# A three-stage model on one core: a third tile for queries and keys, the first load in two parts, four stores begun by GpSimd

## The chip, the cores and the metric

One core of a Trainium2 chip runs the whole program. The metric is the device time of an execution in microseconds; the time given is the median of the runs. One further execution was taken by the profiler; times with a position ("at 20.11") are microseconds from the start of its span.

## What is computed

Attention with a soft cap, then a feed-forward network with a LayerNorm ahead of it, then a gated network that mixes positions. Batch 4, 12 heads of 64, 448 positions, width 768, all float32:

```python
scores = cap * tanh(q @ k.T / 8 / cap)            # 448 x 448 for each of 48 heads
x   = softmax(scores) @ v                          # heads side by side: 4 x 448 x 768
x   = x + relu(layernorm(x) * g @ w_ch1) @ w_ch2   # 768 -> 3072 -> 768
u, v = halves(relu(x @ w_in))                      # 768 -> 1024
out = (u * (w_spatial @ layernorm(v) + b_spatial)) @ w_out
```

## The kernel before, in words

Two heads are worked on together, a "pair"; the program names it by its first head, so 0, 2, 4 and so on. For each pair there is one load of transposed queries and keys (`emit_load`, line 822: 128 rows, of which each head has 64, by 896 columns, queries in columns 0 to 447, keys behind) and two of values (`emit_load_v`, line 836). The pool of tiles for queries and keys, `qk`, has `FIRST[1]` = 2 tiles (line 47).

The lead is the attention of the first two batch elements, 12 pairs, in the first 100 us or so. `lead_s` (line 875) makes the scores of a pair in three groups of 128 keys, `two` and `t` in PSUM, and ScalarE turns them to `e` by a tanh and an exponential. `lead_st` (line 895) makes the last 64 keys of two pairs together. `lead_v` (line 906) multiplies `e` by the values and makes the sums over the keys: VectorE adds the groups of `e` to `es`, TensorE multiplies `es` by `onesr` and `sel`. `invert` (line 1001) takes the sums through DRAM to a shape of 128 rows (`sum`, then `rc`), VectorE takes reciprocals, and they go out and come back, spread over rows (`inv`, then `hs`); VectorE then multiplies `x` by `hs`. When the six pairs of a batch element are there, their LayerNorm follows, which begins with `bank<-wh,onesr` on TensorE; GpSimd takes a power there, with the constant `mhalf`.

Beside the lead, four rows of the first FFN matrix (`EARLY`, line 73) are made ready: `make` (723) calls `weight` (795), which calls `value` (738). A row is loaded as 64-bit words (`w`, two tiles), converted to float32 in four operations by VectorE, or three and one of ScalarE (`wr`, two tiles), stored to DRAM for later use (`kept_w`, line 753), and split in two parts of fewer bits (`rs` or `wh`). The other rows, and the second pair of batch elements, follow behind the lead, as do the two networks, most of the 1008.6 us.

No instruction stands where the code has it. All calls go through `Recorder`, which puts down for each operation its engine, a cost and, for a transfer, a latency (line 544, for SP alone, whose name here is "D"); line 561 issues it at last, so that all rows of the profile name L561. `order` (327) gives each operation a due time from TensorE's order and the costs, and `plan` (374) runs a list schedule with these costs and sets the order on every engine. Operations under `at_once` (the first loads, lines 1863 to 1867) come ahead of all others.

Of the kernel before, what the change touches and what calls it, by code (L numbers as in the profile page):

```python
# [43 lines left out]
FAST = 22,  # L44

COUNTS = 16, 10, 3, 2, 3, 1
FIRST = 2, 2, 2, 1
REST = 7, 10
LEAD = 2, 5

# [173 lines left out]
class Program:  # L224
# [102 lines left out]
    def order(self):  # L327
        n = len(self.ops)
        pred = self.edges()
        self.pred, self.succ = pred, [[] for _ in range(n)]  # L330
        for i, ds in enumerate(pred):
            for j, at in ds.items():
                self.succ[j].append((i, at))
        self.bufs = []
        for i, (_, writes, reads) in enumerate(self.ops):
            mine = list(dict.fromkeys(a.buf for a in chain(writes, reads) if isinstance(a, View)))
            for b in mine:
                b.first = i if b.first is None else b.first
                b.last = i
                b.uses += 1  # L340
            self.bufs.append(mine)
        self.pools = {b.pool for m in self.bufs for b in m}
        total = 0.0
        due = [float("inf")] * n
        for i in range(n):
            engine, cost = self.ops[i][0][0][:2]
            if engine == "PE":
                due[i] = total
                total += cost
            elif i in self.soon:  # L350
                due[i] = total
        for p in self.pools:
            p.reuse()
        for s in self.stages:
            begins = [b for p in s.pools for b in p.bufs if b.first is not None]
            if s.after and begins:
                first = min(begins, key=lambda b: b.first)
                for a in s.after:
                    for b in (b for p in a.pools for b in p.bufs if not b.after):
                        assert b.last < first.first  # L360
                        b.gates.append(first)
        for i in reversed(range(n)):
            engine, cost, latency = self.ops[i][0][0][:3]
            latency += 1.4 if engine == "D" else 0.0
            for j, at in chain(self.succ[i], {(a.first, 0.0) for b in self.bufs[i] for a in b.after},
                               {(a.first, -OPEN / SLACK) for b in self.bufs[i] for a in b.gates}):
                due[i] = min(due[i], due[j] + at * SLACK - (cost + latency + self.DELAY) * SLACK)
            if due[i] == float("inf"):
                due[i] = total
        for i in self.first:  # L370
            due[i] = float("-inf")
        return self.plan(due)

    def plan(self, due):
# [14 lines left out]
        out = []  # L389
# [59 lines left out]
        while True:  # L449
            for e in ready:  # L450
                if busy[e]:
                    continue
                found = pick(e)
                if found is None:
                    continue
                i, k = found
                taken[i] = True
                out.append((i, k))
                for b in bufs[i]:
                    if b.tile is None:  # L460
                        b.pool.take(b)
                busy[e] = True
                cost, latency = self.ops[i][0][k][1:3]
                if e == "PE":
                    spent += cost
                free[e] = now + cost
                if e == "D":
                    moved = max(moved, now + 1.5) + latency
                    latency = moved + 0.77 - now - cost
                heapq.heappush(events, (now + cost, 0, seq, e))  # L470
                done = now + cost + latency + self.DELAY
                for j, at in succ[i]:
                    heapq.heappush(events, (max(now, done - at), 1, seq, j))
                    seq += 1
                heapq.heappush(events, (done, 2, seq, i))
                seq += 1
            if not events:
                rest = [d for q in ready.values() for d, i, _ in q if not taken[i] and d > reach()]
                if not rest:
                    break  # L480
                relief = min(rest)
                continue
            relief = float("-inf")
            now, kind, _, x = heapq.heappop(events)
            if kind == 0:
                busy[x] = False
            elif kind == 1:
                left[x] -= 1
                if not left[x]:
                    release(x)  # L490
            else:
                for b in bufs[x]:
                    b.left -= 1
                    if not b.left:
                        b.pool.give(b)
                        if b.pool.stage is not None and not b.pool.stage.left:
                            for s in b.pool.stage.then:
                                if not s.open and all(not a.left for a in s.after):
                                    s.open = True
                                    out.append((s, None))  # L500
                                    for p in s.pools:
                                        p.changes += 1
                                    for p in s.more:
                                        p.idle.extend(p.late)
                                        p.changes += 1
# [16 lines left out]
class Recorder:  # L522
# [3 lines left out]
    def __getattr__(self, method):  # L526
        fn = getattr(self.engine, method)

        def put(a):
            return a.place() if isinstance(a, View) else a  # L530

        def record(*args, **kw):
            out = kw["out"] if "out" in kw else args[0]
            ins = [a for a in list(args) + list(kw.values()) if hasattr(a, "tensor") and a is not out]
            n = out.free_size()
            latency = 0.0
            psum_in = any(a.space == bass.MemoryType.PSUM for a in ins)
            if self.name == "PE":
                cost = (n / 2400 + 0.0133) * kw["rhs"].ap[0][1] / 128
                if kw["rhs"].dtype == F32:  # L540

                    part = kw["rhs"].ap[0][1] * kw["out"].ap[0][1] / 128 ** 2
                    cost = (4 * n / 2400 + 0.004) * part + (0.004 if part < 1 else 0.0)
            elif self.name == "D":
                cost, latency = 0.5, 4 * out.size() / 360e3
            elif self.name == "A":
                cost = (0.13 if psum_in else 0.16) + n / 1200
                cost += 0.094 if hasattr(kw.get("scale"), "tensor") else 0.0
            elif self.name == "P":
                cost = 1.3 if "pow" in repr(args) + repr(kw) else 0.7 + n / 500  # L550
            elif method == "reciprocal":
                cost = 0.15 + n / 160
            elif method in ("tensor_copy", "tensor_scalar") and not psum_in:
                cost = 0.14 + n / 1920
            else:
                cost = 0.14 + n / 960
            if self.name == "V":
                cost += 0.06 * sum(hasattr(kw.get(k), "tensor") for k in ("scalar", "scalar1", "scalar2"))

            def call():  # L560
                fn(*(put(a) for a in args), **{k: put(a) for k, a in kw.items()})  # L561

            self.program.add(self.name, cost, latency, call, [out], ins)

        return record
# [3 lines left out]
def attn_ffn_gmlp_kernel(  # L569
# [168 lines left out]
    def value(kind, j, home=None, pool=wr):  # L738
# [5 lines left out]
        elif (kind, j) in kept:  # L744
            t = pool.get()[:, 0:n]
            SP.dma_start(out=t, in_=kept[kind, j])
        else:
            raw = raw6[0].get()[:, 0:n]
            SP.dma_start(out=raw.rearrange("p n t -> p (n t)"), in_=source[kind][j].bitcast(I32))
            t = pool.get()[:, 0:n]  # L750
            convert(t, raw, home is None, kind in ("wv", "wu", "wo"))
            d = kept[kind, j] = dram.tile([128, n], F32, name=f"kept_{kind}_{j}")
            SP.dma_start(out=d, in_=t)
        return t

    def block(q, g, pool, early):
# [65 lines left out]
    def emit_load(i):  # L822
# [3 lines left out]
        b, h = heads[i]  # L826
        t = raws[i] = qks.get()

        SP.dma_start(out=t, in_=qk[b, h:h + 2].rearrange("a p n -> (a p) n")[64:192])

    def place(i):

# [1029 lines left out]
    def main():  # L1862
        with prog.at_once():
            emit_load(0)
            SP.dma_start(out=capt, in_=cap)
            emit_load(2)
            emit_load_v(0)
        SP.dma_start(out=g_t, in_=g_ln)
# [101 lines left out]
```

## Time and profile before

| | |
|---|---|
| median of 3 runs | 1011.92 us (1008.72 to 1013.71) |
| the profiled execution | 1010.37 us |
| its span, first to last instruction | 1008.6 us |
| TensorE, busy | 997.3 us |
| VectorE, ScalarE, GpSimd, busy | 855.2, 584.9, 16.7 us |
| granted clock of TensorE | 1.000 of 2.4 GHz all through |

Engines: PE is TensorE (PEld its weight loads), DVE VectorE, ACT ScalarE, POOL GpSimd, SPq the queue of SyncE, which starts transfers. A row of the timeline gives start, length, engine, line, operation, what is written from what, and how many; in brackets the idle time of the engine ahead of it and what ended it. A matrix product in float32 shows as two matmuls. Overlapped operations of an engine are shown with their whole length, so that the distance between two starts can be less than the length.

### The profile page before, as it was taken

How to read it: one execution, taken by the hardware profiler on the slowest of the kernel's cores; microseconds unless marked ns; L12 is line 12 of the kernel's file. 1: busy time of each engine (PE TensorE's matmuls, PEld its weight loads, DVE VectorE, ACT ScalarE, POOL GpSimd, SP SyncE). 2: the span in 40 equal slices, each digit the busy share in tenths (PEclk: the TensorE clock that was granted, in tenths of full speed). 3: DMA queues.
4: the chain of work that ended last, by engine and by line, in shares of the span. 5: the costliest groups of instructions: out<-in, count | busy, mean ns of one | idle time of the engine just before them, and what ended most of it. 6: DMA issues, size and time to landing. Idle time of an engine off the chain costs nothing.

```text
span 1008.6 us, 14721 instructions
## 1 busy us (share of the span) xinstructions
PE 997.3 (99%) x5108; PEld 827.7 (82%) x5108; DVE 855.2 (85%) x1425; ACT 584.9 (58%) x890; POOL 16.7 (2%) x22
## 2 busy tenths in 40 slices
PE   8999999999999999999999999999999999999998
PEld 2334787787788899998989889999999999998987
DVE  6767887888967899989889999877788988968996
ACT  7996955877775358656356355444453543314653
POOL 0000000000000000000000200000000000000010
PEclk9999999999999999999999999999999999999999
DMA  7546678988897998997386233565699857302402
GB/s 251 170 137 180 214 254 294 365 305 303 300 331 230 347 359 297 332 345 273 119 308 218 43 144 116 169 204 191 236 329 371 290 184 233 103 21 71 128 21 110
DMA packets 121197, 224.30 MB, mean 222 GB/s; under 512 B 20594, under 2 KB 83236, under 8 KB 121124
## 3 DMA queue, kind: packets, MB, share of 16 engines
q1 hardware_dynamic: 121124, 223.38, 65.1%
q8 instruction: 40, 0.66, 0.3%
q14 instruction: 33, 0.27, 0.1%
HBM read 152.76 MB, written 70.57 MB: 221 GB/s over the span
## 4 chain that ended last, share of the span: by engine, by line
PE 84%; DMA 6%; DVE 6%; issue 1%; ACT 1%; SPq 1%; DVEq 0%; ACTq 0%
PE bank L561 58%; PE two L561 26%; DMA w6m<-in_w_dram 2%; DVE rs L561 1%; DVE x L561 1%; DMA hs<-inv 1%; DMA std<-var_t 1%; DVE wh L561 1%; DMA w<-in_w_dram 1%; SPq L561 1%; PE t L561 1%; DVE qkg L561 1%; DMA wq<-kept_w 1%; DMA qk<-in_qk_dram 1%; DVE wr L561 1%
## 5 line engine op out<-in xcount | busy, mean ns | idle before, releaser
L561 PE MATMUL bank<-rs,wh 128*128 128x448 f32 x1728 | 362.9, 363 | 1.2 <-DVE rs L561 0.7
L561 PEld LDWEIGHTS bank<-rs,wh 128*128 128x128 f32 x1728 | 322.5, 187 | 29.5 <-issue 3.0
L561 PE MATMUL two<-rs,wh 128*128 128x448 f32 x462 | 103.7, 362 | 0.7 <-DVE wh L561 0.7
L561 DVE TENSOR_TENSOR rs<-hs,rs 128x448 fp32r<-128x448 f32 x159 | 94.3, 618 | 4.7 <-ACT rs L561 4.5
L561 ACT ACTIVATE rs<-hs 128x448 fp32r<-128x448 f32 x135 | 73.2, 570 | 32.7 <-DMA hs<-h 31.4
L561 PEld LDWEIGHTS two<-rs,wh 128*128 128x128 f32 x462 | 86.5, 187 | 6.9 <-DVE wh L561 1.0
L561 DVE TENSOR_TENSOR wh<-wr,wh 128x768 fp32r<-128x768 f32 (+2 forms) x66 | 57.4, 871 | 3.0 <-ACT wh L561 2.5
L561 ACT ACTIVATE hs<-bank 128x448 f32<-128x448 f32 x58 | 31.5, 543 | 40.1 <-PE bank L561 33.9
L561 ACT ACTIVATE wh<-wr 128x768 fp32r<-128x768 f32 (+2 forms) x44 | 33.7, 766 | 30.8 <-PE bank L561 16.6
L561 ACT ACTIVATE es<-es,capt 128x896 f32<-128x896 f32 x42 | 42.6, 1052 | 0.1
L561 ACT ACTIVATE hx<-bank 128x448 f32<-128x448 f32 x30 | 16.3, 543 | 39.2 <-PE bank L561 30.1
L561 PE MATMUL two<-qk 64*128 64x448 f32 (+1 forms) x168 | 36.1, 575 | 2.9 <-DMA qk<-in_qk_dram 2.0
L561 ACT ACTIVATE rs<-x 128x448 fp32r<-128x448 f32 x29 | 16.3, 575 | 36.5 <-DVE x L561 35.1
L561 PE MATMUL bank<-es,vt 128*64 128x448 f32 (+1 forms) x192 | 36.0, 551 | 0.0
L561 ACT ACTIVATE es<-two,qsc 128x896 f32<-128x896 f32 x32 | 31.5, 1007 | 6.3 <-PE two L561 6.3
L561 PE MATMUL two<-wh,rs 128*128 128x512 f32 x144 | 34.7, 389 | 0.0
L561 PE MATMUL bank<-rx,whb 128*128 128x448 f32 x144 | 32.7, 362 | 0.0
L561 PE MATMUL two<-rx,whb 128*128 128x448 f32 x144 | 32.7, 362 | 0.0
L561 DVE TENSOR_TENSOR es<-es,es 128x896 f32<-128x896 f32 x24 | 26.1, 1086 | 7.5 <-ACT es L561 7.5
L561 PEld LDWEIGHTS two<-qk 64*128 64x128 f32 (+1 forms) x168 | 11.3, 173 | 25.5 <-issue 9.1
L561 PEld LDWEIGHTS two<-wh,rs 128*128 128x128 f32 x144 | 27.0, 188 | 5.6
L561 ACT ACTIVATE e<-e,capt 128x2688 f32<-128x2688 f32 (+1 forms) x14 | 31.0, 2224 | 0.2
(268 smaller groups left out, 1966.1 us busy)
## 6 DMA issues: line engine op xcount, KB each, us to landing
hs<-h SPq DMA_DIRECT2D x168, 224.0 KB
h<-hx SPq DMA_DIRECT2D x84, 224.0 KB
w<-in_w_dram SPq DMA_DIRECT2D x24, 768.0 KB
qk<-in_qk_dram SPq DMA_DIRECT2D x24, 448.0 KB
h<-hs SPq DMA_DIRECT2D x48, 224.0 KB
kept_w<-wr SPq DMA_DIRECT2D x24, 384.0 KB
w6q<-in_w_dram SPq DMA_DIRECT2D x12, 768.0 KB
w6m<-in_w_dram SPq DMA_DIRECT2D x12, 768.0 KB
```

The lines of the kernel that those rows point to most:

```text
L561: fn(*(put(a) for a in args), **{k: put(a) for k, a in kw.items()})
```

## The change

The pool `qk` gets a third tile. The first pair's load goes out in two parts, columns 0 to 575 (the queries and the first 128 keys), and the rest, with the load of `cap` between them. The store of a converted row in `value` is begun by GpSimd (`P`) where the row is one of the four early ones (`home` is given), by SP elsewhere as before. The costs of the planner learn of transfers begun by GpSimd: 1.1 us on that engine, and a latency as for SP's.

```diff
-FIRST = 2, 2, 2, 1
+FIRST = 2, 3, 2, 1
...
-            latency += 1.4 if engine == "D" else 0.0
+            latency += 1.4 if latency else 0.0
...
-                if e == "D":
+                if latency:
...
-            elif self.name == "D":
-                cost, latency = 0.5, 4 * out.size() / 360e3
+            elif method == "dma_start":
+                cost, latency = 0.5 if self.name == "D" else 1.1, 4 * out.size() / 360e3
...
-            SP.dma_start(out=d, in_=t)
+            (SP if home is None else P).dma_start(out=d, in_=t)
...
-        SP.dma_start(out=t, in_=qk[b, h:h + 2].rearrange("a p n -> (a p) n")[64:192])
+        x = qk[b, h:h + 2].rearrange("a p n -> (a p) n")[64:192]
+        for r in (slice(0, S + 128), slice(S + 128, 2 * S)) if i == 0 else (slice(0, 2 * S),):
+            SP.dma_start(out=t[:, r], in_=x[:, r])
+            if r.start == 0 and i == 0:
+                SP.dma_start(out=capt, in_=cap)
...
             emit_load(0)
-            SP.dma_start(out=capt, in_=cap)
             emit_load(2)
```

TensorE's instructions stand in the same order as before, all of them. The other engines' differ in the lead alone.

On SP, the first queue of loads, from the second load of weights on; before (`qk_412` and `qk_413` are the two tiles, `w_424` and `w_425` the two tiles of raw weights, `wr_92` the converted row):

```order
L561 DMA w_425<-in_w_dram 128x1536
L561 DMA qk_412<-in_qk_dram 128x896
L561 DMA kept_w_0_142<-wr_92 128x768
L561 DMA w_424<-in_w_dram 128x1536
L561 DMA qk_413<-in_qk_dram 128x896
L561 DMA vt_0_414<-in_v_dram 128x2x192
L561 DMA vt_0_414<-in_v_dram 64x2x64
L561 DMA kept_w_1_145<-wr_93 128x768
```

and now (`qk_412` to `qk_414` are the three tiles, `w_425` and `w_426` the raw weights), from the load of pair 4 on:

```order
L561 DMA qk_414<-in_qk_dram 128x896
L561 DMA vt_0_416<-in_v_dram 128x2x192
L561 DMA w_426<-in_w_dram 128x1536
L561 DMA qk_412<-in_qk_dram 128x896
L561 DMA w_425<-in_w_dram 128x1536
L561 DMA qk_413<-in_qk_dram 128x896
L561 DMA vt_0_415<-in_v_dram 128x2x192
L561 DMA vt_0_415<-in_v_dram 64x2x64
L561 DMA qk_414<-in_qk_dram 128x896
```

The two stores are gone from the queue, and the load of pair 4 stands ahead of the weights' second row, in a tile of its own; the load of pair 6 is the next of `qk_412`.

On VectorE, the adding of the second pair's `e` beside the conversion of the second and third row, with what each waits for; before:

```order
L561 TENSOR_TENSOR es_433<-es_433,e_419 128x896 [waits DVE_49,Activation_49]
L561 TENSOR_TENSOR rs_64<-wr_92,rs_63 128x768 [waits DVE_49]
L561 TENSOR_SCALAR wr_93<-w_425 128x768 [waits DMAHW0_49]
L561 TENSOR_SCALAR wr_93<-wr_93 128x768 [waits DVE_49]
L561 SCALAR_TENSOR_TENSOR wr_93<-w_425,wr_93 128x768 [waits DVE_49]
L561 COPY x_0_113<-bank_138 128x448 [waits PE_49]
L561 SCALAR_TENSOR_TENSOR wr_93<-w_425,wr_93 128x768 [waits DVE_49]
L561 TENSOR_SCALAR wr_92<-w_424 128x768 [waits DMAHW3_49,DMAHW2_49]
L561 CAST rs_65<-wr_93 128x768 [waits DVE_49]
L561 TENSOR_TENSOR es_434<-e_420 128x896 [waits Activation_49]
L561 TENSOR_TENSOR rs_66<-wr_93,rs_65 128x768 [waits DVE_49]
L561 TENSOR_TENSOR es_434<-es_434,e_420 128x896 [waits DVE_49]
```

and now (`e_421` and `es_435` are the second pair's; `DMASW0_49` is the first of GpSimd's stores):

```order
L561 CAST rs_63<-wr_92 128x768 [waits DVE_49]
L561 TENSOR_TENSOR es_434<-es_434,e_420 128x896 [waits DVE_49,Activation_49]
L561 TENSOR_TENSOR rs_64<-wr_92,rs_63 128x768 [waits DVE_49]
L561 TENSOR_SCALAR wr_93<-w_426 128x768 [waits DMAHW2_49]
L561 TENSOR_SCALAR wr_93<-wr_93 128x768 [waits DVE_49]
L561 COPY x_0_113<-bank_138 128x448 [waits PE_49]
L561 SCALAR_TENSOR_TENSOR wr_93<-w_426,wr_93 128x768 [waits DVE_49]
L561 TENSOR_SCALAR wr_92<-w_425 128x768 [waits DMAHW4_49,DMASW0_49]
L561 SCALAR_TENSOR_TENSOR wr_93<-w_426,wr_93 128x768 [waits DVE_49]
L561 TENSOR_TENSOR es_435<-e_421 128x896 [waits Activation_49]
L561 CAST rs_65<-wr_93 128x768 [waits DVE_49]
L561 TENSOR_TENSOR es_435<-es_435,e_421 128x896 [waits DVE_49]
```

The second addition to `es` now stands ahead of the subtraction into `rs_66`, no longer behind it, and the first write of the third row (`wr_92<-w_425`) one place earlier, where it waits for GpSimd's store of the first.

On SP, the transfers of the sums in the middle of the lead, from the sums' second way out on; before:

```order
L561 DMA rc_89<-sum_2_143 128x14
L561 DMA qk_412<-in_qk_dram 128x896
L561 DMA sum_6_146<-hs_80 4x448
L561 DMA inv_2_144<-rc_89 128x14
L561 DMA qk_413<-in_qk_dram 128x896
L561 DMA rc_90<-sum_6_146 128x14
L561 DMA hs_79<-inv_2_144 64x448 x2
```

and now:

```order
L561 DMA sum_6_146<-hs_80 4x448
L561 DMA qk_413<-in_qk_dram 128x896
L561 DMA rc_89<-sum_2_143 128x14
L561 DMA rc_90<-sum_6_146 128x14
L561 DMA qk_414<-in_qk_dram 128x896
L561 DMA inv_2_144<-rc_89 128x14
L561 DMA inv_6_147<-rc_90 128x14
L561 DMA hs_79<-inv_2_144 64x448 x2
```

The two ways back (`rc`) now stand together ahead of the second load of queries and keys. On GpSimd the four stores stand ahead of the memset of `mhalf`, its last operation ahead of the LayerNorm.

## Rows read from the trace of the kernel before

**Rows 1.** The page, part 1: busy us (share of the span) xinstructions.

```profile
PE 997.3 (99%) x5108; PEld 827.7 (82%) x5108; DVE 855.2 (85%) x1425; ACT 584.9 (58%) x890; POOL 16.7 (2%) x22
```

**Rows 2.** Busy time by stretch, then granted clock, DMA share, GB/s.

```profile
4.69:20.11 15.42, 13.56 (x69) 4.39 (x68) 9.75 (x15) 14.02 (x14) 0.00 (x0) 1.00 0.86 301
20.11:59.71 39.60, 38.59 (x217) 12.98 (x217) 29.45 (x42) 37.28 (x34) 0.00 (x0) 1.00 0.57 174
...
69.25:1008.60 939.35, 932.79 (x4763) 806.41 (x4763) 809.29 (x1356) 523.36 (x835) 15.89 (x13) 1.00 0.66 225
```

**Rows 3.** TensorE's waits, 0 to 100 us: total, times, longest.

```profile
PE two L561 <- DMA qk<-in_qk_dram: 2.0, 2, 1.0
...
PE two L561 <- ACT e L561: 0.9, 1, 0.9
PE bank L561 <- DVE x L561: 0.5, 1, 0.5
```

**Rows 4.** Timeline, TensorE: start, us, what, [idle before, releaser].

```profile
4.69 2.06 PE L561 MATMUL two<-qk 64*128 64x448 f32 x8
...
20.11 0.97 PE L561 MATMUL two<-qk 64*64 64x448 f32 x4 [1.01 <-DMA qk<-in_qk_dram]
...
24.37 0.96 PE L561 MATMUL bank<-es,onesr 128*32 128x448 f32 x8
...
59.71 1.02 PE L561 MATMUL two<-qk 64*128 64x448 f32 x4 [1.01 <-DMA qk<-in_qk_dram]
...
68.76 1.01 PE L561 MATMUL bank<-wh,onesr 128*128 128x448 f32 x2 [0.46 <-DVE x L561]
```

**Rows 5.** Chain of waits, 4 to 21 us: start, us, what.

```profile
3.37 7.10 DMA w<-in_w_dram
...
13.68 0.33 SPq L561
...
14.58 5.49 DMA qk<-in_qk_dram
```

**Rows 6.** SP's own waits, 0 to 45 us.

```profile
SPq L561 <- DVE wr L561: 13.4, 4, 4.8
```

**Rows 7.** Timeline, SP: its DMA issues.

```profile
0.73 0.39 SPq L561 DMA_DIRECT2D qk<-in_qk_dram  x1
...
8.45 0.33 SPq L561 DMA_DIRECT2D qk<-in_qk_dram  x1
...
46.73 0.52 SPq L561 DMA_DIRECT2D sum<-hs  x1
...
49.23 0.54 SPq L561 DMA_DIRECT2D rc<-sum  x1
...
55.34 0.34 SPq L561 DMA_DIRECT2D qk<-in_qk_dram  x1
```

**Rows 8.** Timeline, VectorE.

```profile
10.50 0.56 DVE L561 TENSOR_SCALAR wr<-w 128x768 f32<-128x768 f32 x1 [5.34 <-DMA w<-in_w_dram]
...
11.69 1.96 DVE L561 SCALAR_TENSOR_TENSOR wr<-w,wr 128x768 int32<-128x768 int32 x2
...
20.37 0.56 DVE L561 TENSOR_SCALAR wr<-w 128x768 f32<-128x768 f32 x1
...
22.31 0.95 DVE L561 TENSOR_TENSOR rs<-wr,rs 128x768 fp32r<-128x768 f32 x1
...
23.18 1.09 DVE L561 TENSOR_TENSOR es<-es,e 128x896 f32<-128x896 f32 x1
...
45.57 0.24 DVE L561 RECIPROCAL rc<-rc 128x14 f32<-128x14 f32 x1 [4.79 <-DMA rc<-sum]
```

**Rows 9.** Timeline, ScalarE.

```profile
6.05 1.01 ACT L561 ACTIVATE e<-two,qsc 128x896 f32<-128x896 f32 x1 [3.83 <-PE two L561]
...
21.13 1.01 ACT L561 ACTIVATE es<-two,qsc 128x896 f32<-128x896 f32 x1 [0.60 <-PE two L561]
```

**Rows 10.** GpSimd's groups: xcount, busy us, mean ns, idle before.

```profile
L561 POOL TENSOR_TENSOR rstd_t<-var_t,mhalf 112x4 f32<-112x4 f32 x4 | 5.2, 1300 | 308.2 <-DMA var_t<-var 308.2
```

## The prediction

> **What bounds the kernel now.** I read the totals first: TensorE is busy for 997.3 us [rows 1] of a span of 1008.6, so all that any change to waits can win is about 11 us, and the matmuls themselves are not touched by this one. Then the span cut at the moments where TensorE waits: behind 69.25 us it is busy for 932.79 of 939.35, and the change reaches nothing there; between 4.69 and 20.11 it is busy for 13.56 of 15.42, between 20.11 and 59.71 for 38.59 of 39.60 [rows 2]. The waits of TensorE in the first 100 us name the causes: two waits for a load of queries and keys, 1.0 us each, one of 0.9 for ScalarE, and 0.5 for VectorE at the LayerNorm of the first batch element [rows 3]. The timeline puts the first of the two loads at 20.11, the second at 59.71 [rows 4].
>
> The chain of waits tells why the load at 20.11 was late: the first row of the first FFN matrix lands 7.10 us after its issue, VectorE converts it, SP stands at the store of the converted row until 13.68, and the load that is behind the store in SP's queue goes out at 14.58 and takes 5.49 us [rows 5]. The four stores hold SP for 13.4 us in the first 45 [rows 6]. The two loads' causes differ: at 59.71 no store is near. There the load goes out at 55.34, as the last of a chain of small transfers (sums out at 46.73, back in at 49.23, and so on), in each of which SP waits for the transfer before [rows 7].
>
> **The change, part by part.** The order shows that TensorE's instructions keep their order, all of them; only tiles change. What moves is SP's queue, the first fifty or so instructions of VectorE, a few on ScalarE, and four stores that now begin on GpSimd.
>
> *First load in two parts.* The scores' first group needs columns 0 to 575 of 896. The whole load goes out at 0.73 [rows 7] and TensorE starts on it at 4.69 [rows 4], 3.96 us later. A part with 64% of the bytes lands earlier by nothing at least (if latency is all) and by 36% of the 1.5 us that 448 KB take at the 300 GB/s seen in [rows 2], 0.55 us, at most. I take 0.3, between the ends. The second part can be up to 1.5 us late: ScalarE reads its scores only after the tanh and the exponential of the first group, a good 2 us after 6.05 [rows 9]. The price is one more issue ahead of the weights, about 0.4 us as SP's other issues [rows 7]; that moves the start of VectorE's conversion, now 10.50 [rows 8], by 0 to 0.4. I take 0.2.
>
> *Third tile.* Pair 4 gets a tile of its own, so that the load of pair 6 is the one issued when the first tile comes free, as at 8.45 now [rows 7], and no longer behind a store. It has 11 us until TensorE wants it, and the slowest load here took 5.5 [rows 5]. The wait of 1.01 at 20.11 goes, and with it ScalarE's idle 0.60 [rows 9]. With the 0.3 of the first load TensorE is then 1.3 us early.
>
> *What is late next.* The matmuls of the row sums start at 24.37 [rows 4], and the addition that they need runs on VectorE from 23.18 for 1.09, to 24.27 [rows 8]: today both come together, so VectorE would hold TensorE back as soon as that is early. VectorE is without a gap from 10.50 on, and does not start earlier. But one operation, the subtraction of the second row, now stands behind that addition and no longer ahead of it: from its start to the addition's is 23.18 - 22.31 = 0.87 [rows 8]. Less the 0.2 of the later weights, the row sums start 0.67 earlier. Of 1.3 us 0.67 pass; the rest becomes a wait for VectorE.
>
> *Four stores on GpSimd.* SP loses four issues and the waits ahead of them. What is queued behind them on GpSimd is one small memset for the first LayerNorm, wanted much later. A store's issue from GpSimd is not in this trace; between SP's 0.33 [rows 5] and a small operation of GpSimd, 1.30 us [rows 10], I take the upper. Who waits for it: VectorE's first write of the third row, into the tile that the first store reads. Now this is at 20.37; in the new order it stands one operation earlier, half of the 1.96 of two such, so at about 19.4 [rows 8]. The tile was done at 13.66 (two operations from 11.69, 1.96 us). The store's landing has no row either; bounded by the quickest contended load of that size, 4.3 us from 55.34 [rows 7] to 59.71 [rows 4], and the slowest, 5.49 [rows 5], it is through at 13.66 + 1.30 + 4.3 = 19.3 or at 20.5. So the wait is 0 to 1.1 us. I take 0, as the SP queue is relieved of that store: the total traffic stays the same. At 1.1 the whole 0.67 would be gone.
>
> *What 59.71 does with the gain.* This load stays behind the same small transfers, so the 0.67 is worth nothing unless the chain of these is earlier too. It begins when a copy of sums follows VectorE's reciprocal at 45.57, which today waits 4.79 us for a transfer that SP issued late, behind a load [rows 8]; in the new order the two re-layouts of sums stand together ahead of that load. By my count along SP's queue (a transfer of sums 2.5 us from 46.73 to 49.23, as today, and the issues of some 0.5 between) the load goes out at about 54.7, 0.6 before 55.34; with 0 and 1.2 as ends, as one or two issues more or less stand ahead. So TensorE passes this point 0.6 us earlier and still waits. The LayerNorm of 68.76 hangs on the same chain; I give it nothing more.
>
> **Sum:** 0.6 us at the point where all of the lead has to pass, though about 1.9 us of waits are touched ahead of it. The profiled execution, 1010.37, would come to 1009.8. It stands below the median of the three runs, 1011.92 (1008.72 to 1013.71); the middle of the four executions is 1011.1, and I set the prediction there less 0.6: **1010.5**.
>
> **The rivals.** *Full gain.* SP is free of 13.4 us of waiting [rows 6], so the sums could come by more than I count, and both loads, the 0.3 at the start and the 0.46 of the LayerNorm go: 0.3 + 1.01 + 1.01 + 0.46 = 2.8, which gives 1008.4. For it: each is a transfer in SP's queue. Against: VectorE without a gap, and a chain in which each link waits for the landing before it. Chance 0.25.
>
> *The gain does not come.* The wait for VectorE at 24.37 or the chain behind 46.73 takes all back: 1011.1. For it: the margin of the store is 0.1 us by one bound. Chance 0.2.
>
> *Slower: VectorE holds up the store that it waits for.* If GpSimd cannot begin a store while VectorE works on data in SBUF, then the first store starts only when VectorE comes to a stop, which is at the write that waits for that store, at 19.4: VectorE would stand for 1.3 + 4.3 = 5.6 us, of which 0.67 were won, and TensorE would lose 4.9 at 24.37: 1016.0. It decides from a landing later than 19.4 + 0.67 = 20.1. For it: VectorE has no gap there, and moves 768 columns in 0.56 us with one input and needs 0.95 with two [rows 8], so the quick form may hold something that GpSimd needs too. Against: only a third of VectorE's time between 13.66 and 19.4 is the quick form. The Trainium skill states this mechanism (SBUF — State Buffer, section "SBUF: two separate sides"): a DMA begun on GpSimd needs descriptors which GpSimd writes over a port pair that VectorE's quick forms lock, each for its whole length. No row before shows it. By that rule as written, with the three quick operations that the order has between 13.66 and 19.4 (a CAST, two TENSOR_SCALAR), the store would be late by up to 3 x 0.56 = 1.7, and the time 1011.5 to 1012. Chance of the slow case 0.1.
>
> The forecast itself, a gain of 0.3 to 1.2, has the remaining 0.45.
>
> **How the numbers follow.** A measurement of this kernel can tell about 0.5%, 5 us, as its three runs lie 5.0 apart. None of the cases but the last reaches that: faster by over 0.5% would be under 1006.9, which takes the full gain and a low run besides: 0.08. Slower, over 1017.0, takes the slow case and a high run: 0.06. Within: 0.86. The range reaches down to 1007.2, the full gain with a run 1.2 below it, and up to 1013.8, about the highest run of before: no gain with the scatter of a run above it, or half of the slow case's loss (1011.1 + 2.5).
>
> **What would show it.** Right: TensorE starts near 4.4; no wait for a load at 20; a wait of some 0.6 for VectorE's addition at about 23.7; the load of 59.71 issued near 54.7, with a wait of 1 us left. The first store's landing against VectorE's write at 19.4 decides the slow rival: a wait for a DMA of the stored row on VectorE would show it. Wrong: no wait at 59, or any wait of several us on VectorE ahead of 24; or a TensorE that has other busy time than 997, since its work does not change.

## The result and the profile after

The changed kernel takes 1016.5 us (median of 7 runs, 1013.92 to 1021.0), the kernel before 1009.75 beside it (7 runs, 1008.67 to 1013.71): ratio 1.0062, 95% interval 1.0042 to 1.0082. It is slower by some 6 us, more than the 0.5% that can be told; the prediction was 1010.5, within 1007.2 to 1013.8. The profiled execution has 1016.5 us too, with a span of 1014.7, 6.1 longer than before.

The page's totals of the changed kernel, answering to [rows 1], say that the engines do nearly the same work:

```profile
PE 999.6 (99%) x5108; PEld 828.0 (82%) x5108; DVE 856.0 (84%) x1426; ACT 584.2 (58%) x889; POOL 19.4 (2%) x26
```

TensorE has 2.3 us more, GpSimd 2.7, for the most part the four stores that it now issues. TensorE's waits in the first 100 us, to be held against [rows 3]:

```profile
PE bank L561 <- DVE x L561: 3.6, 2, 3.3
...
PE bank L561 <- DVE es L561: 1.0, 2, 0.5
PE two L561 <- ACT e L561: 0.9, 1, 0.9
```

Both waits for a load of queries and keys, 2.0 us, are gone. In their place stands one wait of 3.3 for VectorE's `x`. The timeline of TensorE in the changed kernel says where (start, us, what; idle time before it and what ended it), as [rows 4] before:

```profile
4.70 1.77 PE L561 MATMUL two<-qk 64*128 64x448 f32 x8
...
24.18 0.57 PE L561 MATMUL bank<-es,onesr 128*32 128x448 f32 x2 [0.48 <-DVE es L561]
...
58.37 1.02 PE L561 MATMUL two<-qk 64*128 64x448 f32 x4
...
65.81 0.57 PE L561 MATMUL bank<-es,onesr 128*32 128x448 f32 x2 [0.52 <-DVE es L561]
...
71.77 1.00 PE L561 MATMUL bank<-wh,onesr 128*128 128x448 f32 x2 [3.35 <-DVE x L561]
72.70 3.14 PE L561 MATMUL two<-qk 64*128 64x448 f32 x8
75.62 1.30 PE L561 MATMUL t<-qk 64*128 64x448 f32 x4
76.85 2.48 PE L561 MATMUL bank<-e,vt 128*64 128x448 f32 x12
```

At 58.37 TensorE is 1.34 us ahead of the 59.71 of [rows 4]: the third tile does what it should. Then the lead goes. The sums at 65.81 wait for VectorE, and the LayerNorm's first matmul, 68.76 before, stands at 71.77, 3.01 late, with 3.35 of idle time ahead of it. The three rows behind it in the kernel before are

```profile
69.70 1.77 PE L561 MATMUL two<-qk 64*128 64x448 f32 x8
71.31 0.92 PE L561 MATMUL t<-qk 64*128 64x448 f32 x4
72.16 2.48 PE L561 MATMUL bank<-e,vt 128*64 128x448 f32 x12
```

so that the same eight matmuls take 3.14 instead of 1.77. The stretches of the changed kernel (us, busy time of PE, PEld, DVE, ACT and POOL, granted clock, DMA share, GB/s) tell the reason:

```profile
70.00:72.00 2.00, 0.23 (x1) 0.19 (x1) 1.93 (x5) 0.00 (x0) 0.00 (x0) 1.00 0.68 144
72.00:74.00 2.00, 1.94 (x6) 0.83 (x7) 1.97 (x3) 1.20 (x2) 0.00 (x0) 0.74 0.57 206
74.00:76.00 2.00, 2.00 (x8) 1.04 (x6) 2.00 (x5) 1.41 (x3) 0.00 (x0) 0.50 0.00 0
76.00:78.00 2.00, 2.00 (x10) 0.48 (x8) 2.00 (x6) 1.89 (x2) 0.00 (x0) 0.90 0.06 11
...
76.85:1014.70 937.85, 930.22 (x4752) 804.97 (x4750) 804.81 (x1349) 519.84 (x831) 16.18 (x13) 1.00 0.66 224
```

Behind the idle time the granted clock falls from 1.00 (2.4 GHz) to 0.50 (1.2 GHz). From the LayerNorm's matmul to the next product with the values it is 76.85 - 71.77 = 5.08, before 72.16 - 68.76 = 3.40: the clock costs 1.68, most of TensorE's 2.3. The 6.1 us are then 3.01 at the LayerNorm, 1.68 of clock, and 1.41 in all that follows (937.85 from 76.85 on; before, 1008.6 - 72.16 = 936.44).

**Why the LayerNorm is late** stands in SP's queue. Its issues in the changed kernel, to be held against [rows 7]:

```profile
8.17 0.33 SPq L561 DMA_DIRECT2D qk<-in_qk_dram  x1
...
32.54 0.60 SPq L561 DMA_DIRECT2D sum<-hs  x1
33.26 3.14 SPq L561 DMA_DIRECT2D vt<-in_v_dram  x2
38.41 0.54 SPq L561 DMA_DIRECT2D sum<-hs  x1
39.05 0.38 SPq L561 DMA_DIRECT2D qk<-in_qk_dram  x1
39.52 0.89 SPq L561 DMA_DIRECT2D rc<-sum  x2
41.02 0.33 SPq L561 DMA_DIRECT2D qk<-in_qk_dram  x1
42.88 0.80 SPq L561 DMA_DIRECT2D inv<-rc  x2
46.54 1.78 SPq L561 DMA_DIRECT2D hs<-inv  x3
48.41 0.51 SPq L561 DMA_DIRECT2D sum<-hs  x1
...
57.43 0.49 SPq L561 DMA_DIRECT2D sum<-hs  x1
```

The first sums (pairs 0 and 2) go out at 32.54, but their way back, `rc<-sum`, starts only at 39.52. SP is through with two loads of values at 33.26 + 3.14 = 36.40, and then the second sums (pairs 4 and 6) stand ahead of it in the queue. Those are copied out of PSUM late; in this kernel ScalarE does it:

```profile
37.87 0.52 ACT L561 ACTIVATE hs<-bank 128x448 f32<-128x448 f32 x1
```

and SP's own waits between 30 and 60 us of the changed kernel name it:

```profile
SPq L561 <- ACT hs L561: 2.0, 1, 2.0
```

From there each transfer waits for the landing of the one before, and the third sums (pair 8), 46.73 in [rows 7], go out at 48.41. At the end VectorE, in the changed kernel, waits for the spread reciprocals of the last pairs, twice, and the additions to `es` that TensorE's sums at 65.81 need stand in order behind the first wait:

```profile
62.35 0.63 DVE L561 TENSOR_TENSOR x<-x,hs 128x448 f32<-128x448 f32 x1 [2.83 <-DMA hs<-inv]
...
64.67 1.09 DVE L561 TENSOR_TENSOR es<-es,e 128x896 f32<-128x896 f32 x1
69.47 0.62 DVE L561 TENSOR_TENSOR x<-x,hs 128x448 f32<-128x448 f32 x1 [3.71 <-DMA hs<-inv]
```

The order at this place, on SP, of the kernel before:

```order
L561 DMA sum_2_143<-hs_79 4x448
L561 DMA vt_0_415<-in_v_dram 64x2x64
L561 DMA vt_0_415<-in_v_dram 128x2x192
L561 DMA rc_89<-sum_2_143 128x14
```

and of the changed one:

```order
L561 DMA sum_2_143<-hs_79 4x448
L561 DMA vt_0_416<-in_v_dram 64x2x64
L561 DMA vt_0_416<-in_v_dram 128x2x192
L561 DMA sum_6_146<-hs_80 4x448
L561 DMA qk_413<-in_qk_dram 128x896
L561 DMA rc_89<-sum_2_143 128x14
L561 DMA rc_90<-sum_6_146 128x14
```

That is a reading of two traces. The experiments ask whether this order costs the time, which part of the change made it, and whether the stores or the tile have a hand in it.

### The profile page after: what moved, and what is told of

Its sections match the earlier page's. It is cut to its first block, busy times and chain, and to the rows that moved or that the text cites. A ratio compares the mean times of both kernels' runs of the same rounds, so it can differ in the third digit from the quotient of the medians.

```text
span 1014.7 us, 14721 instructions
## 1 busy us (share of the span) xinstructions
PE 999.6 (99%) x5108; PEld 828.0 (82%) x5108; DVE 856.0 (84%) x1426; ACT 584.2 (58%) x889; POOL 19.4 (2%) x26
## 5 line engine op out<-in xcount | busy, mean ns | idle before, releaser
L561 DVE TENSOR_TENSOR x<-x,hs 128x448 f32<-128x448 f32 x30 | 17.6, 622 | 16.6 <-DMA hs<-inv 15.0
```

## The experiments

Each time is a median, each ratio one to runs of the kernel before on the same chip, with its 95% interval.

**First: which part of the change.** Four kernels. `order_only` keeps the changed kernel's order on all engines, but starts the first load in one piece:

```diff
             SP.dma_start(out=t[:, r], in_=x[:, r])
+            if i == 0:
+                prog.ops[-1][0][0][3][:] = [] if r.start else [lambda: nc.sync.dma_start(out=t.place(), in_=x)]
```

> The change with its new order of instructions on all engines, but the first load in one piece again. Theory A (the planner's new order of the small transfers of the sums makes the LayerNorm late, the transfers themselves do not matter): as the changed kernel, LayerNorm matmul near 71.8 us of the span with about 3 us of waiting, clock below 1 after it, 1014 to 1018 us. Theory B (the third tile's loads stand in the rings ahead of the small transfers): the same, 1014 to 1018. Theory C (the two parts of the first load themselves): as before or better, 1008 to 1010.

`no_split` takes the load in two parts out of the plan as well:

```diff
-        for r in (slice(0, S + 128), slice(S + 128, 2 * S)) if i == 0 else (slice(0, 2 * S),):
+        for r in (slice(0, 2 * S),):
```

> The change without the two parts, planned as such: third tile and stores on GpSimd stay, the order of VectorE and ScalarE is that of the kernel before. Theory A: the sums go out and back as before or earlier, the LayerNorm matmul starts at 69.3 us or earlier, no wait over 1 us, clock 1, both waits for loads gone: 1006.5 to 1009.5. Theory B: the loads of three tiles are still there, the LayerNorm stays near 71.8: 1013 to 1017. Theory D (the stores on GpSimd hold VectorE): 1013 to 1017.

`split_quiet` starts two parts, of which the planner knows nothing (it sees one load):

```diff
-        for r in (slice(0, S + 128), slice(S + 128, 2 * S)) if i == 0 else (slice(0, 2 * S),):
-            SP.dma_start(out=t[:, r], in_=x[:, r])
-            if r.start == 0 and i == 0:
-                SP.dma_start(out=capt, in_=cap)
+        SP.dma_start(out=t, in_=x)
+        if i == 0:
+            one, two = (lambda r=r: nc.sync.dma_start(out=t[:, r].place(), in_=x[:, r])
+                        for r in (slice(0, S + 128), slice(S + 128, 2 * S)))
+            prog.ops[-1][0][0][3][:] = [one]
+            SP.dma_start(out=capt, in_=cap)
+            prog.ops[-1][0][0][3].append(two)
```

> The first load goes out in two parts with the cap between, but the planner does not see it: all other instructions stand as in the run without the parts. Theory A: as that run or a few tenths earlier, 1006.5 to 1009.5. Theory B and D: 1013 to 1017. Theory C: like the changed kernel, 1014 to 1018.

`no_third` is the changed kernel with two tiles:

```diff
-FIRST = 2, 3, 2, 1
+FIRST = 2, 2, 2, 1
```

> The change with two tiles for queries and keys, the order of VectorE, ScalarE and GpSimd unchanged. Theory A: the sums stand as late as in the changed kernel, 1014 to 1018. Theory B: the loads are where they were, the sums come as before, 1008 to 1011.

| kernel | us | ratio | LayerNorm's matmul, wait before it |
|---|---|---|---|
| order_only | 1015.71 | 1.0046 [1.0029, 1.0063] | 72.06, 2.51 |
| no_split | 1012.47 | 1.0016 [0.9998, 1.0034] | 69.17, 1.87 |
| split_quiet | 1011.37 | 0.9995 [0.9976, 1.0014] | 71.36, 3.53 |
| no_third | 1015.24 | 1.0040 [1.0024, 1.0056] | 72.40, none noted |

The order alone costs what the change costs, within the intervals; the two parts, with the order that the planner makes without them, cost nothing that can be told. So the planner's answer to the two-part load brings the loss, not the transfers. `order_only` and `no_third` came out where Theory A had them. `no_split` and `split_quiet` are free of the loss, but both missed its 1006.5 to 1009.5: neither is faster than the kernel before. `no_third` has that order as well, and with it the loss, although its wait is another one, in its timeline:

```profile
62.24 1.86 PE L561 MATMUL two<-qk 64*128 64x448 f32 x4 [3.83 <-DMA qk<-in_qk_dram]
```

With two tiles the load stands behind the late sums, and TensorE waits 3.83 for it; with three it waits 3.35 at the LayerNorm. That load went out at 58.12, 2.8 later than the 55.34 of [rows 7]. One late chain, two places where it shows. `split_quiet` is not as clean as its time would have it. Its profiled execution of 1012.30 us was nearly as late at the LayerNorm as the changed kernel, and its clock fell to 0.50 as well:

```profile
71.36 1.00 PE L561 MATMUL bank<-wh,onesr 128*128 128x448 f32 x2 [3.53 <-DVE x L561]
...
76.44 2.48 PE L561 MATMUL bank<-e,vt 128*64 128x448 f32 x12
```

The product behind the LayerNorm is 4.28 us later than the 72.16 of the kernel before; all that follows took 2.4 less than there, won back between 311 and 546. One profile is one execution, and a late lead alone does not make a long one.

**Second: the stores, and the place of the LayerNorm.** `pool_alone` makes one part of the change, the stores on GpSimd, with two tiles and one load:

```diff
-FIRST = 2, 3, 2, 1
+FIRST = 2, 2, 2, 1
...
-        for r in (slice(0, S + 128), slice(S + 128, 2 * S)) if i == 0 else (slice(0, 2 * S),):
+        for r in (slice(0, 2 * S),):
```

> Only the stores on GpSimd, two tiles, first load in one piece. Theory A: order of VectorE and ScalarE as before, the sums as early as before, the wait for the load at 20 us shorter or gone, the one near 59 still there: 1009 to 1012. Theory D (GpSimd's stores cost by themselves): VectorE waits for a store by over a microsecond and TensorE with it: 1013 to 1016.

It took 1010.71, ratio 1.0003 [0.9985, 1.0021]: the stores neither cost nor bring anything that can be told. TensorE's waits for loads were 0.7 in all; the LayerNorm stood at 70.09.

If the lateness of the sums is the cost, a LayerNorm that TensorE reaches later should be free of it. `after_ln_later` and `no_split_ln_later` move its place three groups of scores on:

```diff
-LN_AT = 4.2
+LN_AT = 6.0
```

> The changed kernel with the LayerNorm's matmul of the first batch element three groups of scores later in TensorE's order (its due time 6.0 instead of 4.2). Theory A (the sums come late, TensorE stands at this matmul, and its clock falls after it): TensorE does 2.5 us of scores in the meantime, the wait falls from 3.3 to 1 us or less, the clock stays at 1, the lag behind the kernel before, 4.7 us at the end of this stretch, falls to about 1: 1010 to 1013 us. Rival (the time is lost elsewhere, the wait only shows it): 1014.5 to 1018.

> Third tile and stores on GpSimd, first load in one piece, LayerNorm's matmul three groups later. Theory A: the wait of 1.9 us that the run without the later LayerNorm had goes, nothing waits for loads: 1.5 to 2 us below that run, 1008 to 1011 us. Rival: another wait in the lead takes its place: 1011 to 1014.

They took 1016.86 (1.0065 [1.0043, 1.0087]) and 1017.33 (1.0065 [1.0045, 1.0084]). Both missed: the due times move with the place, the planner set the other engines anew, and the operand came as late as 73.5 and 72.7. They do not answer the question, as too much moved; in SP's queue both have the second sums ahead of the first `rc<-sum`, as the changed kernel has. They show a planner at work on a small input once more: the second kernel lost 4.9 us against `no_split` by one number.

`after_filled` should separate the clock from the wait, by sixteen matmuls whose product nobody reads, ahead of the LayerNorm's:

```diff
+        if b == 0:
+            hi = made["w1", 0][0]
+            hi = hi.rearrange("p k n -> p (k n)")[:, 0:S]
+            o = prog.ops[-1][0][0]
...
+            o[3][:0] = [lambda: nc.tensor.matmul(out=ps.place(), lhsT=onesr[:], rhs=hi.place(), start=True, stop=True)
+                        for _ in range(16)]
```

> The changed kernel with 16 matmuls that compute nothing wanted, some 3 us, ahead of the LayerNorm's matmul, into the bank that it overwrites; the order of all else is the same. If the fall of the clock after the wait of 3.35 us is a cost of its own, the clock stays at 1 and the scores behind the LayerNorm take 3.4 us to the next group instead of 5.1: about 1.7 us faster than the changed kernel, 1013 to 1016. If the clock falls anyway, or its fall costs nothing, 1015.5 to 1018.

It took 1020.20 (1.0089 [1.0058, 1.0119]), more than either case had. The added matmuls write the bank of the LayerNorm, and that was not yet free, so that they stood idle themselves, as its timeline shows:

```profile
73.21 5.88 PE L1139 MATMUL bank<-rs,onesr 128*128 128x448 f32 x16 [4.00 <-DVE x L561]
```

and then ran at the low clock. No work covered the wait; the split between clock and wait rests on the rows of the section above, not on this run.

**Third: is it SP's queue at all?** In three kernels the transfers of the sums of the first batch element start on GpSimd, while the plan stays as it was, so that SP holds none of them up:

```diff
+        Q = Recorder(prog, "D", nc.gpsimd) if name[0] == "0" else SP
-        SP.dma_start(out=d0, in_=rows)
-        SP.dma_start(out=c, in_=packed(d0))
+        Q.dma_start(out=d0, in_=rows)
+        Q.dma_start(out=c, in_=packed(d0))
...
-        SP.dma_start(out=packed(d1), in_=c)
+        Q.dma_start(out=packed(d1), in_=c)
...
-            SP.dma_start(out=o, in_=d1[j:j + 1].partition_broadcast(64))
+            Q.dma_start(out=o, in_=d1[j:j + 1].partition_broadcast(64))
```

> The changed kernel with the transfers of the first batch element's sums (out, back, reciprocals out, back spread) issued by GpSimd and no longer by SP; planned as before, so that the order on the other engines is the changed kernel's, word for word. Theory A (in SP's queue the sums stand behind loads and their waits): the LayerNorm matmul starts before 70.5 instead of 71.8, its wait is under 2 us, the clock stays at 1: 1009 to 1013 us. Rival E (the sums are slow because each small transfer takes 2 to 3.5 us to land, whoever issues it): it stays near 72: 1014 to 1018.

> The same with the first load in one piece. Theory A: the LayerNorm matmul, 69.2 in that run with a wait of 1.9, comes at 67.5 to 68 without a wait, so 1 to 2 us less than that run: 1008.5 to 1011.5 us. Rival E: as that run or, as a transfer that GpSimd issues takes longer to issue (0.54 us against 0.33), up to 2 us slower: 1012 to 1015.

> The kernel before with the sums' transfers issued by GpSimd and nothing else changed. Theory A: the LayerNorm's wait of 0.46 goes, the load at 59.7 is no longer behind the sums in SP's queue and its wait of 1.0 goes as well: 1008 to 1010, 0.5 to 1.5 us less than the kernel before. Rival E: 1010 to 1013.

They took 1020.89 (1.0090 [1.0062, 1.0117]), 1020.04 (1.0078 [1.0051, 1.0106]) and 1018.33 (1.0072 [1.0050, 1.0094]), four executions each; one of the first kernel's took 2011.76, its other three 1019.43 to 1022.21. The LayerNorm stood at 76.14, 76.06 and 74.43. All three are slower than either theory had, and even the kernel before lost 7 us. On GpSimd each issue of the sums took 0.53 to 0.77 us where SP needs 0.32 to 0.61, and the queue there still goes in order: the copies wait for each other as on SP. That speaks against the plain idea that SP is too full. It does not speak against an order in which one link of the chain stands behind a later one, since that order was kept.

**Fourth: the order itself.** Two kernels are the changed one with all its edits, where after planning some instructions are put back. `sp_order_back` changes the order of fifteen transfers of SP's queue and nothing else (`sum_2`, `sum_6` and `sum_8` are the first, second and third sums going out, `rc_2` is `rc<-sum_2`, `inv_2` its reciprocals going out, `vt` a load of values):

```diff
-sum_6 qk_413 rc_2 rc_6 qk_414 inv_2 inv_6 hs hs hs<-inv_2 sum_8 hs<-inv_2 hs<-inv_6 vt vt
+rc_2 qk_413 sum_6 inv_2 qk_414 rc_6 hs hs hs hs<-inv_2 inv_6 sum_8 vt vt hs<-inv_6
```

> The changed kernel, all engines as they stand in it, with one thing put back: the order of fifteen transfers in SP's queue between the first copy of sums and the load of the values of pair 6 (rc<-sum_2 again ahead of sum_6, inv_2 ahead of rc<-sum_6 and of the load of queries and keys, the four hs<-inv_2 together). Theory A, the place of the sums in SP's queue costs the time: sum_8 goes out at about 46.8 instead of 48.4, the LayerNorm's matmul stands at 69 to 70 instead of 71.8, the time is 1010 to 1013, no slower than before by over 0.3%. Theory B, the order of VectorE and ScalarE costs it (sum_6 waits for a copy of ScalarE that before was VectorE's): sum_6 still goes out at 38.4 or later, LayerNorm at 71 to 72.5, time 1015 to 1017.

`va_order_back` leaves SP as the change has it, and puts VectorE and ScalarE back, the copy of the second sums to VectorE among them (`hs_2`, and four others that change the engine):

```diff
-A: wh_0<-wr_2   V: wr_3<-w6_3   V: wh_1<-wr_3   A: hs_2<-bank_5   V: acc<-x0_0
+V: wh_0<-wr_2   A: wr_3<-w6_3   A: wh_1<-wr_3   V: hs_2<-bank_5   A: acc<-x0_0
```

> The counterpart: the changed kernel with SP's queue as it stands in it, and the order and the shares of VectorE and ScalarE put back to what they were before (43 instructions of VectorE, 16 of ScalarE; five change the engine back). Theory A: rc<-sum_2 still stands behind sum_6, LayerNorm at 71 to 72.5, time 1015 to 1017. Theory B: LayerNorm at 69 to 70, time 1010 to 1013. If both kernels come out near 1013 to 1014, each order costs a part; if both stay at 1016, neither alone pays and only the two together do.

| kernel | us | runs | ratio |
|---|---|---|---|
| sp_order_back | 1012.28 | 12 | 1.0016 [0.9997, 1.0036] |
| va_order_back | 1017.69 | 6 | 1.0067 [1.0050, 1.0085] |

This settles it between the two orders: with SP's put back the ratio is that of `no_split`, 1.0016; with VectorE's and ScalarE's it is the changed kernel's, and the two intervals lie apart. Which of the fifteen transfers does it was not taken apart further. In `va_order_back` the copy of the second sums is VectorE's again, and SP stands as long for it as for ScalarE's, 1.9 against 2.0 (SP's waits between 30 and 60, then its issues):

```profile
SPq L609 <- DVE hs L609: 1.9, 1, 1.9
```

```profile
33.63 0.60 SPq L609 DMA_DIRECT2D sum<-hs  x1
...
39.42 0.54 SPq L609 DMA_DIRECT2D sum<-hs  x1
...
40.53 0.91 SPq L609 DMA_DIRECT2D rc<-sum  x2
...
49.35 0.51 SPq L609 DMA_DIRECT2D sum<-hs  x1
```

while in `sp_order_back` the first `rc<-sum` follows its sums by 3.9 us, not 6.9:

```profile
33.70 0.62 SPq L609 DMA_DIRECT2D sum<-hs  x1
...
37.61 0.45 SPq L609 DMA_DIRECT2D rc<-sum  x1
...
40.15 0.55 SPq L609 DMA_DIRECT2D sum<-hs  x1
...
47.72 0.53 SPq L609 DMA_DIRECT2D sum<-hs  x1
```

The time from the first sums' start to the third's goes the same way, by a small margin, in the profiles that have the stores on GpSimd and the first sums by themselves on SP: 15.9 in the changed kernel, 16.5 in `order_only`, 15.7 in `no_third` and in `va_order_back`, 15.5 in `after_filled` (medians of 1015.2 to 1020.2 us); 13.7 in `no_split`, 14.0 in `sp_order_back`, 13.9 in `sums_sooner` below, 15.1 in `pool_alone`, 14.8 in `split_quiet` (1010.4 to 1012.5 us). The order parts the kernels better: wherever SP issues the sums, the first `rc<-sum` stands behind the second sums in every kernel of 1015.2 us and more, the two with the later LayerNorm among them, and ahead of them in every kernel of 1012.5 us and less, the kernel before among them.

What the profile of `sp_order_back` does not show is the lead won back. It was profiled in one of its longest executions (1017.75 of 1009.34 to 1019.13), with the LayerNorm late, where 69 to 70 was expected, and a fall of the clock:

```profile
70.84 1.09 PE L609 MATMUL bank<-wh,onesr 128*128 128x448 f32 x2 [2.21 <-DVE x L609]
...
75.88 2.48 PE L609 MATMUL bank<-e,vt 128*64 128x448 f32 x12
```

That product is only 0.97 ahead of the changed kernel's 76.85. With the same order of the sums and the first load in one piece it does come early: at 72.56 in `no_split`, 73.47 in `pool_alone`, 71.57 in `sums_sooner`; the two late ones, this and `split_quiet`, both start the load in two parts. The three executions of `sp_order_back` with a mean granted clock of 0.997 or 0.998 took 1017.75, 1017.96 and 1019.13, the nine at 0.999 or 1.000 took 1009.34 to 1013.31. In the changed kernel all seven had 0.995 to 0.998; but so had five of `split_quiet`'s ten (0.998), and those took 1010.21 to 1012.48. So the times show that SP's order costs some 0.5%. That it does so through the lateness at 72 us is read from the changed kernel's trace, and the profiles of `sp_order_back` and `split_quiet` do not confirm it: whether the two parts by themselves make the lead late in some executions was not tested.

**Fifth: the chain moved forward.** If the chain of the sums decides, then the last sums of the batch element, sooner, must give time back. `sums_sooner` is `no_split` with five transfers of SP in another order and one reciprocal of VectorE moved, again after planning:

```diff
-hs<-inv_8 sum_10 qk_412 hs<-inv_8 rc_10 qk_413 inv_10
+sum_10 hs<-inv_8 hs<-inv_8 rc_10 qk_412 qk_413 inv_10
...
-x_4<-x_4,hs rc_10<-rc_10
+rc_10<-rc_10 x_4<-x_4,hs
```

> The kernel with the third tile and GpSimd's stores, first load in one piece (no wait for loads there; its LayerNorm waited 1.87 us), with the last sums of the batch element sooner: in SP's queue sum_10 and rc<-sum_10 go ahead of two loads and of an hs<-inv_8, and VectorE's reciprocal of them ahead of the product that waits for hs<-inv_8. By the rows of that kernel rc<-sum_10 goes out at about 56.1 instead of 57.5, inv_10 at 59 instead of 61.2, so that the LayerNorm's matmul is ready some 2 us sooner. Theory (chain of the sums sets the lead): LayerNorm at 67.0 to 67.8 with a wait under 0.5, time 1.5 to 2 us below that kernel's, about 1009 to 1010.5 and 0 to 2 us below before. Rival (the lead is lost again behind it, or the chain is bound elsewhere): 1011.5 to 1013, as that kernel.

```profile
58.02 0.33 SPq L609 DMA_DIRECT2D inv<-rc  x1
...
68.18 1.00 PE L609 MATMUL bank<-wh,onesr 128*128 128x448 f32 x2 [1.60 <-DVE x L609]
```

`inv_10` goes out at 58.02 (in `no_split` 61.22), the LayerNorm stands at 68.18 with a wait of 1.60, a microsecond earlier, and not the two that were expected. Most of that microsecond is not the order's: this execution was 0.72 ahead already at the first scores behind 57 (57.99 against 58.71). Of the 3.2 us at `inv_10` little arrives, since the transfer now stands right behind two loads and lands after 3.51 us, in `no_split` after 1.81. The time is 1010.43 (12 runs), ratio 0.9995 [0.9980, 1.0010], 0.67% under the changed kernel by the two ratios. It is 2 us under `no_split`, as expected, but the two intervals overlap, so that a gain by the moved sums is not shown; nor is it faster than the kernel before by anything that can be told.

## Why the prediction was wrong

**The step that failed** is the one on 59.71: "This load stays behind the same small transfers", and behind it "The LayerNorm of 68.76 hangs on the same chain; I give it nothing more." The load does not stay there. With a third tile it goes out at 41.02, not at the forecast 54.7, and its wait is gone whole. And the chain is not 0.6 earlier; it is late, at the third sums by 48.41 - 46.73 = 1.68, at the LayerNorm by 3.01. I saw in the order that "the two re-layouts of sums stand together ahead of that load" and took that as a gain. It was the loss: they stand together because the first had been put behind the second sums, which wait for their copy. I counted issues, and did not ask of each what it waits for. Two of the prediction's own signs of being wrong came with it: no wait at 59, and another busy time of TensorE, 999.6.

**The start.** TensorE's first scores do not start near 4.4 but at 4.70; a gain of 0.3 shows one step later, ScalarE's first tanh at 5.77 against 6.05 [rows 9], though one profile each cannot tell so little.

**The wait at 20.11** is gone, as forecast.

**VectorE at 24.** A wait for its addition was forecast at 23.7 with 0.6; it stands at 24.18 with 0.48. VectorE started at 10.03, not 0.2 later but 0.47 earlier than in [rows 8], and lost that again to the first store:

```profile
20.23 0.56 DVE L561 TENSOR_SCALAR wr<-w 128x768 f32<-128x768 f32 x1 [1.23 <-DMA kept_w<-wr]
...
23.05 1.08 DVE L561 TENSOR_TENSOR es<-es,e 128x896 f32<-128x896 f32 x1
```

The addition, forecast 0.67 earlier than 23.18, came 0.13 earlier: 0.87 by the new order and 0.47 by the early start, less the 1.23.

**The store** came just outside its bounds of 0 to 1.1 us of wait: 1.23, where I took 0. The bounds came from loads of 448 KB, the quicker of them 4.37 by the rows named, not 4.3; the store has 384 KB. The first store was issued at 13.49 in 0.74 us (1.30 had been taken), and needed longer to land than the 4.3 to 5.5 that the bounds had. The four stores' view gives

```profile
13.49 0.74 POOL L561 DMA_DIRECT2D kept_w<-wr  x1 [12.16 <-DVE wr L561]
21.97 0.55 POOL L561 DMA_DIRECT2D kept_w<-wr  x1 [7.74 <-DVE wr L561]
...
DMA to landing us min/median/max: 2.6/3.5/6.7
```

**The slow rival** had named 1016.0, and the result is 1016.5, but by another mechanism. VectorE waited 1.23 for a store, not 5.6, and TensorE, 0.2 ahead at 24.18, lost by it most of the 0.67 that it was to win there, but nothing against before. The Trainium skill (SBUF — State Buffer, section "SBUF: two separate sides") has stores begun on GpSimd starve while VectorE's quick forms run. The traces bear that out in no clear way. The first store landed at 13.49 + 6.7 = 20.2, 1.2 us after VectorE had come to a stop at 19.0, so it had not waited for that stop to begin: the quickest of the four took 2.6. Its 6.7 us would fit the prediction's estimate of up to 1.7 lost by that rule; it would also fit the loads beside it, with which the DMA engines were busy nearly all the time (share 0.97 from 4.70 to 20.11). Which of them it was is not settled. The other three landed in 2.6 to 3.9 beside a VectorE with as few gaps, and `pool_alone` has the stores and no loss.

**Not foreseen at all** was the clock. At a wait of 3.35 us the price is not the wait alone; 1.68 came on top, behind 69.25, where by the prediction "the change reaches nothing". I held every wait of before to be about one microsecond, and none of them moves the clock [rows 2].

**What stays open.** Of the 6.1 us of the two profiles 1.41 lie behind 76.85 and have no cause here. That part, with the same matmuls in it, is 936.44 in the kernel before, 934.06 in `split_quiet` and 940.02 in `sp_order_back`, so it moves by more than the 1.41 from profile to profile. By which path SP's order costs the time in the median execution is open, as these two profiles have a late lead and one of them a short time. Why the planner puts `rc<-sum` behind the second sums when the first load is in two parts was not traced through its costs; the runs show only that it does, and what it costs. The third tile with the stores, without the two parts, comes out at 1.0016, an interval that includes no change: the tile's gain at both loads is there on the timeline, and lost at the LayerNorm's wait of 1.87.

## What to carry to other kernels

Where a planner sets the order, a small edit's cost lies in what the planner does with it: read the new order on each queue, and at each instruction that has moved, ask what the instruction now ahead of it waits for. A transfer that returns a result, put behind one that must wait for another engine, delayed every link of its chain here. And where the gain of a change is a few waits of a microsecond, the next chain can decide; here the loads' waits turned whole into one longer wait at the LayerNorm.

## What the runs showed of the hardware that was not expected

TensorE's granted clock fell to 0.50 after an idle time of 3.35 us and the work behind it cost 1.68 us more. After 3.53 idle in `split_quiet` and 2.21 in `sp_order_back` it fell too, at nearly the same price (5.08 and 5.04 us from the LayerNorm to the next product, in the kernel before 3.40); after 2.51 in `order_only` it did not (75.45 - 72.06 = 3.39 from the LayerNorm to the next product). The Trainium skill (TensorE: Matmul & The Clock Gate, section "HAM oscillation — how this bites in real kernels") says that waits for transfers between groups of matmuls bring the clock down and that the next group starts at the lower level; the trace agrees, and shows besides that the length of the wait alone does not decide.

A store of 384 KB begun by GpSimd held that engine for 0.54 to 0.74 us, less than a small operation of it, 1.30 [rows 10]. For the small transfers of the sums GpSimd was the worse queue here: moved there, they cost 7 us in the kernel before.

The start of the lead varies between executions where the code is the same: the first eight score matmuls took 1.77 us in the changed kernel and 2.79 in `sp_order_back`, which has the same load in two parts, and 2.06 in the kernel before and 3.19 in `no_split`, which have it in one. A gain of 0.3 us there is not to be read from one profile each.
